# Layer norm on three engines and sooner, in the output stage of a spectral mixer

## The chip, the cores and the metric

The kernel runs on one core of one Trainium2 chip. The metric is the device time of one execution in microseconds. A median over several executions is given; the profile is of one execution, with its own time.

## The reference

Two layers, each of a spectral mixer (A) and a channel MLP (B), on one sequence of 2048 rows by 576 columns:

```python
def _A_ref(x, w_r, w_i):
    X = rfft2(x.astype(float32), axes=(-2, -1))
    X = X * (w_r + 1j * w_i)
    return irfft2(X, s=(S, D)).astype(bfloat16)

def _B_ref(x, w1, b1, w2, b2):
    y = _layernorm(x)                       # over the 576 columns
    h = gelu(einsum("bsd,df->bsf", y, w1) + b1)   # 4608 wide
    return einsum("bsf,fd->bsd", h, w2) + b2

for _ in range(2):
    x = x + _A_ref(_layernorm(x), A_w_r, A_w_i)
    x = x + _B_ref(_layernorm(x), B_w1, B_b1, B_w2, B_b2)
```

The part that concerns us is the seam between the mixer and the MLP: the last step of the inverse transform gives the new x, tile by tile, and the MLP's first matrix product wants the layer norm of the first 512 rows of that x, transposed.

## The kernel before

The 2048 rows lie in SBUF as 16 tiles of 128 partitions and 576 columns (`x_sb`). The tiles are worked in four quads, `QUADS = [[j, j+4, j+8, j+12] for j in range(4)]`, and `order` lists the tiles quad after quad. The output stage numbers them n = 0 to 15 in that order, so the first quad is n = 0 to 3.

Every engine executes its instructions in the order in which the program lists them (`manual_schedule`); nothing reorders them. What an engine does is therefore decided by the order of the calls in `SpectralOut.run_all`. That stage occurs twice, once in each layer. For each n it issues, in this order:

- `put_x(n)`, only for n = 6 and 10 (n = 1 and 2 are done ahead): TensorE adds x itself into PSUM with four matmuls (L753). These four tiles are called early.
- `idft_k(n)`: six matmuls of 288 columns (L765), into a PSUM tile `psb` of which there are three (tag "big").
- `add(n)`: VectorE forms the new x. For an ordinary tile it is one "even" add of 576 columns (L785), which writes a float32 tile `tt`, and two "odd" adds of 288 columns (`add_odd`, L793 and L794), which write x and after which the PSUM tile is free. The odd adds of tile n-1 follow the even add of tile n, unless n is early. For an early tile ScalarE copies half of the PSUM tile (L777) and VectorE makes two adds (L779).
- what `behind_add[n]` lists,
- `idft_v(n + 2)`: four matmuls (L698) and a ScalarE copy from PSUM (L705), for the tile after next; once in four tiles also `idft_v_rest` (L738, L745),
- what `pieces[n]` lists.

`Prep` is the layer norm of the first quad, which is worked while the later tiles are still being added. `sum(i, k)` are eight ScalarE passes (L845) that accumulate the sum and the sum of squares of tile i. `moments` are three small VectorE instructions (L854 to L856), `root` one ScalarE square root (L860), `scale_sums` two small VectorE instructions (L865, L866). `norm(i)` is one VectorE instruction of 576 columns (L887) that writes `xn`, and `norm_act(i)` the same on ScalarE (L874). Each is followed by a copy of the last 64 columns behind the 576 (L890 on VectorE, L877 on POOL), so that five transposes of 128 columns fill the width. There are three `xn` buffers. `turn(i, "act")` makes five transposes on TensorE (L907) into a PSUM tile `pss`, and one ScalarE copy of 640 columns (L909) to `yT`.

The `pss` tiles (tag "sm") number two. `idft_v`, `idft_v_rest` and `turn` take them in turn, so a transposition can begin only when the ScalarE copy of the last but one user has ended.

The lists before:

```python
pieces[10].append(prep.root)
for i, m in enumerate((13, 14, 14)):
    pieces[m].append(lambda i=i: prep.turn(i, "act"))
behind_add = {9: [prep.moments], 11: [prep.scale_sums, lambda: prep.norm(0, nc.vector)], 12: [lambda: prep.norm(2, nc.vector)]}
pieces[12].append(lambda: prep.norm_act(1))
pieces[13].append(lambda: prep.norm_act(3))
...
    if n == NT - 1:
        prep.turn(3, "act")
```

After n = 15, `mlp_up` begins: matmuls of 512 columns (L931) that read `yT` of all four tiles, and PSUM tiles of the same three `psb` that the adds of tiles 13, 14 and 15 have to free. POOL (GpSimd) issues the exchange DMAs of the stage before, the 64-column copies, one memset for the next mixer (L1122, first layer alone) and the loads of w2 (L265), the latter only after the MLP's first activations.

Of the kernel before, what the change touches and what calls it, by code (L numbers as in the profile page):

```python
# [11 lines left out]
ALU = mybir.AluOpType  # L12
BF16 = mybir.dt.bfloat16
# [4 lines left out]
S, D = 2048, 576  # L18
P = 128
NT = 16  # L20
# [141 lines left out]
def kernel(  # L162
# [12 lines left out]
    nc = tc.nc  # L175
# [8 lines left out]
    work = ctx.enter_context(tc.tile_pool(name="work", bufs=2))  # L184
# [24 lines left out]
    def at(buf, shape, off=0):  # L209
        n = int(np.prod(shape[1:]))  # L210
        dims = "abcd"[: len(shape) - 1]
        return buf[0 : shape[0], off : off + n].rearrange(f"p ({' '.join(dims)}) -> p {' '.join(dims)}", **dict(zip(dims[1:], shape[2:])))

    x_sb = persist.tile([P, NT, D], BF16, name="x_sb")
# [123 lines left out]
    def ln_scale(mv, mlp, sqrt):  # L338

        n = mv.shape[1]  # L340
        rs = work.tile([P, n], F32, tag="ln_rs", bufs=4)
        if sqrt:
            sq = work.tile([P, n], F32, tag="ln_v")
            nc.scalar.activation(
                out=sq[:], in_=mv[:, :, 1], func=ACT.Sqrt, bias=c_eps[:, 1:2] if mlp else c_eps[:, 0:1], scale=(1.0 + EPS) if mlp else 1.0
            )
            nc.vector.reciprocal(out=rs[:], in_=sq[:])
            return [(mv[:, i, 0:1], rs[:, i : i + 1]) for i in range(n)]
        vv = work.tile([P, n], F32, tag="ln_v")
        hv = work.tile([P, n], F32, tag="ln_hv")  # L350
        tt = work.tile([P, n], F32, tag="ln_t")
        sc, add = (1.0 + EPS, EPS * EPS) if mlp else (1.0, EPS)
        nc.vector.tensor_scalar(out=vv[:], in0=mv[:, :, 1], scalar1=sc, scalar2=add, op0=ALU.mult, op1=ALU.add)
        nc.vector.tensor_scalar(out=hv[:], in0=vv[:], scalar1=-0.5, scalar2=None, op0=ALU.mult)
        nc.vector.tensor_scalar(
            out=rs[:].bitcast(I32), in0=vv[:].bitcast(I32), scalar1=-0.5, scalar2=1597463007.0, op0=ALU.mult, op1=ALU.add
        )
        for _ in range(3):
            nc.vector.tensor_mul(out=tt[:], in0=rs[:], in1=rs[:])
            nc.vector.tensor_mul(out=tt[:], in0=tt[:], in1=hv[:])  # L360
            nc.vector.scalar_tensor_tensor(out=rs[:], in0=tt[:], scalar=1.5, in1=rs[:], op0=ALU.add, op1=ALU.mult)
        return [(mv[:, i, 0:1], rs[:, i : i + 1]) for i in range(n)]
# [321 lines left out]
    class SpectralOut:  # L684
# [84 lines left out]

        def add(self, n):  # L770

            if n > 0 and n - 1 not in self.early and n in self.early:
                self.add_odd(n - 1)
            if n in self.early:
                xr, po = x_sb[:, order[n], :].rearrange("p (h n) -> p h n", h=2), self.st.pop(("po", n))
                odd = at(self.sums, [P, DH], 2 * DH * (n % 3))
                nc.scalar.copy(out=odd, in_=po[:, 1, 0:DH])  # L777
                for half, op in ((0, ALU.add), (1, ALU.subtract)):
                    nc.vector.tensor_tensor(out=xr[:, half], in0=po[:, 0, 0:DH], in1=odd, op=op)  # L779
                return  # L780
            if n < NT:
                t, po = order[n], self.st["po", n]
                tt = at(self.sums, [P, 2, DH], 2 * DH * (n % 3))
                xr = x_sb[:, t, :].rearrange("p (h n) -> p h n", h=2)
                nc.vector.tensor_tensor(out=tt, in0=po[:, 0:1, 0:DH].to_broadcast([P, 2, DH]), in1=xr, op=ALU.add)  # L785
                self.st["tt", n] = tt
            if n > 0 and n - 1 not in self.early:
                self.add_odd(n - 1)

        def add_odd(self, n):  # L790
# [5 lines left out]
        def run_all(self, prep, loads):  # L796

            pieces = {n: [] for n in range(NT)}
            for n, (i, k) in zip((1, 2, 3, 4, 5, 5, 6, 7), ((i, k) for i in range(4) for k in range(2))):
                pieces[n].append(lambda i=i, k=k: prep.sum(i, k))  # L800
            pieces[10].append(prep.root)
            for i, m in enumerate((13, 14, 14)):
                pieces[m].append(lambda i=i: prep.turn(i, "act"))
            behind_add = {9: [prep.moments], 11: [prep.scale_sums, lambda: prep.norm(0, nc.vector)], 12: [lambda: prep.norm(2, nc.vector)]}
            pieces[12].append(lambda: prep.norm_act(1))
            pieces[13].append(lambda: prep.norm_act(3))
            for n in self.early[:2]:
                self.put_x(n)
            for n in range(N_FIRST):
                self.idft_v_late(n)  # L810
            self.idft_v_rest_late()
            self.idft_v(0)
            for call in loads:
                tc.add_manual_dep(call(), marks["u2", 0].name, SYNC, reason="pace of the loads")
            self.idft_v(1)
            self.idft_v_rest(0)
            self.idft_v(2)
            for n in range(NT):
                if n == NT - 1:
                    prep.turn(3, "act")  # L820
                if n in self.early[2:]:
                    self.put_x(n)
                self.idft_k(n)
                self.add(n)
                for call in behind_add.get(n, ()):
                    call()
                if 0 < n < NT - 2:
                    self.idft_v(n + 2)
                if n % 4 == 1 and n + 3 < NT:
                    self.idft_v_rest(n // 4 + 1)  # L830
                for call in pieces[n]:
                    call()
            self.add(NT)

    class Prep:
# [35 lines left out]
        def norm_act(self, i):  # L871
            rs, shift = self.rs_shift
            xn = work.tile([P, 640], BF16, tag="xn", bufs=3)
            nc.scalar.activation(  # L874
                out=xn[:, 0:D], in_=x_sb[:, self.quad[i], :], func=ACT.Identity, bias=shift[:, i : i + 1], scale=rs[:, i : i + 1]
            )
            nc.gpsimd.tensor_copy(out=xn[:, D:640], in_=xn[:, D - 64 : D])  # L877
            self.st[i] = xn
# [185 lines left out]
    for n, (kind, j) in enumerate(early):  # L1064
        i = 1 + 5 * n // 8
# [21 lines left out]
    for li in range(N_LAYERS):  # L1087
# [24 lines left out]
        prep = Prep(0, sqrt=True)  # L1112
# [47 lines left out]
```

## Time and profile before

| what | us |
|---|---|
| median of 3 runs | 730.78 (730.43 to 731.42) |
| the profiled execution: its own time | 730.14 |
| the profiled execution: span from first to last instruction | 728.4 |
| TensorE busy in the span | 716.3 (98%) |
| ScalarE busy / VectorE busy / POOL busy | 309.3 / 266.9 / 79.3 |
| layer 0: first L765 matmul, first L931 matmul | 61.52, 84.82 |
| layer 1: L931 matmul after the output stage | 439.61 |

Span and time of the profiled execution differ by 1.7 us, which lies around the instructions. In the profile's rows the name left of `<-` is what is written and the names right of it what is read; the bracket at the end of a row gives the engine's idle time before it and what ended it. Matmuls are pipelined, so their duration reaches beyond the start of the next; the spacing of starts is what a matmul costs. PE is TensorE and PEld its weight load, DVE is VectorE, ACT is ScalarE, POOL is GpSimd, SP the engine that issues DMAs.

In the trace, n = 9 to 15 of layer 0 are psb_1330, 1371, 1395, 1418, 1441, 1468 and 1499, and psb_1513 is the first of the MLP.

### The profile page before, as it was taken

The numbers are of one execution on the slowest core, as the hardware profiler recorded it, in microseconds if no ns is written. First come the engines' busy times: TensorE is split into PE (matmuls) and PEld (weight loads), VectorE is DVE, ScalarE is ACT, GpSimd is POOL, SyncE is SP. The second block draws the span as 40 slices with busy tenths as digits, with TensorE's granted clock in tenths as the row PEclk, the third lists the DMA queues.
The fourth block names the chain that finished last, engine by engine and source line by source line (L and its number), as shares of the span: only waits on it lengthen the run. The fifth ranks groups of instructions, "written<-read, shape, count | busy, mean of one in ns | idle before, by whom it ended". The sixth has DMA issues, their size and how long they took to land.

```text
span 728.4 us, 12438 instructions
## 1 busy us (share of the span) xinstructions
PE 716.3 (98%) x5044; PEld 457.1 (63%) x5078; DVE 266.9 (37%) x917; ACT 309.3 (42%) x534; POOL 79.3 (11%) x139
## 2 busy tenths in 40 slices
PE   9999999999999999999999999999999999999998
PEld 5777645864587448744877774477447744774476
DVE  7894910664055504520366586011400140110011
ACT  7796764026411651156216686610550056005600
POOL 4240112002000200000106201200100010000000
PEclk9999999999999999999999999999999999999999
DMA  9787345211112111100217402530102010100000
GB/s 297 209 194 208 135 152 193 65 44 54 37 36 54 55 27 45 46 8 1 59 37 232 140 2 74 191 110 18 44 1 45 17 45 1 45 21 6 1 17 17
DMA packets 52722, 54.33 MB, mean 75 GB/s; under 512 B 31576, under 2 KB 43624, under 8 KB 52664
## 3 DMA queue, kind: packets, MB, share of 16 engines
q1 hardware_dynamic: 43784, 25.99, 13.3%
q0 software_dynamic: 8448, 26.96, 11.7%
q8 instruction: 40, 0.66, 0.4%
q10 hardware_dynamic: 432, 0.58, 0.2%
q14 instruction: 18, 0.15, 0.1%
HBM read 29.31 MB, written 8.59 MB: 52 GB/s over the span
## 4 chain that ended last, share of the span: by engine, by line
PE 95%; ACT 2%; DVE 1%; issue 1%; DMA 0%; ACTq 0%
PE psb_4485 L978 1%; PE psb_3601 L978 1%; PE psb_7498 L978 1%; PE psb_6900 L978 1%; PE psb_6302 L978 1%; PE psb_3472 L978 1%; PE psb_2799 L978 1%; PE psb_1997 L978 1%; PE psb_1758 L978 1%; PE psb_7652 L978 1%; PE psb_7575 L978 1%; PE psb_7183 L978 1%; PE psb_7106 L978 1%; PE psb_7028 L978 1%; PE psb_6585 L978 1%; PE psb_6508 L978 1%
## 5 line engine op out<-in xcount | busy, mean ns | idle before, releaser
L978 PEld LDWEIGHTS <-h_sb 128*128 128x128 bf16 x2304 | 224.9, 98 | 57.8 <-issue 0.2
L931 PEld LDWEIGHTS <-w_sb 128*128 128x128 bf16 x1152 | 109.4, 98 | 142.4 <-issue 17.2
L887 DVE TENSOR_SCALAR xn<-x_sb,mv,rs 128x576 bf16<-128x576 bf16 x24 | 9.4, 427 | 67.0 <-DMA quad_1817<-xn 28.9
L335 DVE BATCH_NORM_STATS2 stats<-x_sb 128x6 f32<-128x288 bf16 x78 | 30.8, 437 | 0.0
L939 PEld LDWEIGHTS <-w1r_sb 64*128 64x128 bf16 x288 | 10.8, 94 | 24.5 <-issue 17.0
L973 DVE TENSOR_TENSOR xb<-x_sb,b_bc 128x576 f32<-128x576 bf16 x32 | 24.0, 749 | 0.0
L890 POOL COPY xn<-xn 128x64 bf16<-128x64 bf16 x24 | 6.4, 266 | 150.8 <-DVE xn L887 150.8
L656 PEld LDWEIGHTS <-h_sb 128*128 128x128 bf16 x160 | 15.4, 97 | 5.3 <-DVE shared_721 L641 0.5
L945 ACT ACTIVATE h_sb<-psb_6062,b_sb 128x512 bf16<-128x512 f32 x2 | 1.3, 684 | 37.9 <-PE psb_6062 L939 37.9
L945 ACT ACTIVATE h_sb<-psb_6660,b_sb 128x512 bf16<-128x512 f32 x2 | 1.3, 684 | 37.8 <-PE psb_6660 L939 37.8
L945 ACT ACTIVATE h_sb<-psb_7258,b_sb 128x512 bf16<-128x512 f32 x2 | 1.3, 684 | 37.8 <-PE psb_7258 L939 37.8
L1001 DVE TENSOR_TENSOR x_sb<-psb_7498,xb 128x576 bf16<-128x576 f32 x1 | 0.8, 759 | 43.4 <-PE psb_7498 L978 43.4
L1001 DVE TENSOR_TENSOR x_sb<-psb_4099,xb 128x576 bf16<-128x576 f32 x1 | 0.8, 757 | 39.5 <-PE psb_4099 L978 39.5
L417 DVE TENSOR_TENSOR xf<-ef 128x256 bf16<-128x256 f32 (+1 forms) x56 | 13.6, 305 | 0.5
L623 PEld LDWEIGHTS <-c_f_84 128*128 128x128 bf16 x108 | 10.4, 97 | 4.6 <-issue 1.6
L1001 DVE TENSOR_TENSOR x_sb<-psb_6900,xb 128x576 bf16<-128x576 f32 x1 | 0.8, 757 | 33.6 <-PE psb_6900 L978 33.6
L1001 DVE TENSOR_TENSOR x_sb<-psb_6302,xb 128x576 bf16<-128x576 f32 x1 | 0.8, 758 | 33.6 <-PE psb_6302 L978 33.6
L504 PEld LDWEIGHTS <-c_k_82 128*128 128x128 bf16 x112 | 10.4, 98 | 2.3
L1001 DVE TENSOR_TENSOR x_sb<-psb_3293,xb 128x576 bf16<-128x576 f32 x1 | 0.8, 758 | 28.7 <-PE psb_3293 L978 28.7
L1001 DVE TENSOR_TENSOR x_sb<-psb_2491,xb 128x576 bf16<-128x576 f32 x1 | 0.8, 757 | 28.7 <-PE psb_2491 L978 28.7
L845 ACT ACTIVATE h_sb<-x_sb 128x576 bf16<-128x576 bf16 x16 | 11.2, 700 | 0.1
L488 PEld LDWEIGHTS <-xT 128*128 128x128 bf16 x96 | 9.2, 97 | 3.1 <-issue 0.7
(1420 smaller groups left out, 1530.5 us busy)
## 6 DMA issues: line engine op xcount, KB each, us to landing
w_sb<-in_B_w_dram SPq DMA_DIRECT2D x16, 288.0 KB
v_sb<-in_B_w_dram POOLq DMA_DIRECT2D x4, 1152.0 KB, 6.1
shared_1511<-in_B_w_dram POOLq DMA_DIRECT2D x2, 1440.0 KB, 7.4
shared_5459<-in_B_w_dram POOLq DMA_DIRECT2D x2, 1440.0 KB, 7.5
out_dram<-x_sb SPq DMA_DIRECT2D x15, 144.0 KB
v_sb<-w_sb POOLq DMA_DIRECT2D x13, 145.0 KB, 4.8
x_sb<-in_A_x_dram SPq DMA_DIRECT2D x3, 576.0 KB
b_sb<-shared_721 POOLq DMA_DIRECT2D x11, 145.0 KB, 5.0
```

The costliest lines, as they stand in the source:

```text
L335: nc.vector.bn_stats(out=stats[:, h, :], in_=x_sb[:, t, h * DH : (h + 1) * DH])
L417: nc.vector.tensor_tensor(out=xf[:, at0 : at0 + 2 * n].rearrange("p (g d) -> p g d", g=2), in0=ef[:, :, first : first + n], in1=ef[:, :, b ...
L488: nc.tensor.matmul(pz[:, o, 0:KP], lhsT=xT[:, ci, :], rhs=c_fd[:, 3 * o + q, :], start=(q == 0), stop=(q == 2),)
L504: nc.tensor.matmul(py[:, r, 0:KP], lhsT=(c_k1_late if t in LATE else c_k1)[:, pl, :], rhs=z[:, ri], start=(q == 0), stop=(q == 1))
L623: nc.tensor.matmul(px[:, o, 0:KP], lhsT=c_f2[:, n // 4, pl, n % 4, :], rhs=vx[:, E_SLOTS.index(e), ri, :], start=(q == 0), stop=(q == 1))
L656: nc.tensor.matmul((ph, odd)[o][:, o, 0:KP], lhsT=i1[:, pl, n % 4, :], rhs=rhs, start=(q == 0), stop=(q == len(terms) - 1))
L845: nc.scalar.activation(out=at(h_sb, [P, D], 512 * 34), in_=x_sb[:, self.quad[i], :], func=(ACT.Copy, ACT.Square)[k], accum_out=self.s12[:, ...
L887: nc.vector.tensor_scalar(out=xn[:, 0:D], in0=x_sb[:, self.quad[i], :], scalar1=mean, scalar2=rs, op0=ALU.subtract, op1=ALU.mult)
L931: nc.tensor.matmul(acc[p][q], lhsT=w1_sb[:, ci, fc * 128 : (fc + 1) * 128], rhs=yT[:, ci, :], start=(first and ci == 0), stop=(not first a ...
L939: nc.tensor.matmul(acc[p][q], lhsT=w1r_sb[rows, p, :], rhs=yT[rows, 4, :], start=first, stop=not first)
L973: nc.vector.tensor_tensor(out=xb[:], in0=xr, in1=b2_bc[:].rearrange("p (h n) -> p h n", h=2), op=ALU.add)
L978: nc.tensor.matmul(parts[h][:, h, 0:DH], lhsT=hts[fc][:, i * 128 : (i + 1) * 128], rhs=w2_chunk(fc)[:, h * DH : (h + 1) * DH], start=(fc = ...
```

## The change

The lists are written anew, a third kind of norm is added, and the odd adds of two late tiles are moved.

```diff
         def add(self, n):
-            if n > 0 and n - 1 not in self.early and n in self.early:
+            odd_first = n in self.early or n >= NT - 2
+            if n > 0 and n - 1 not in self.early and odd_first:
                 self.add_odd(n - 1)
...
-            if n > 0 and n - 1 not in self.early:
+            if n > 0 and n - 1 not in self.early and not odd_first:
                 self.add_odd(n - 1)
...
-            pieces[10].append(prep.root)
-            for i, m in enumerate((13, 14, 14)):
-                pieces[m].append(lambda i=i: prep.turn(i, "act"))
-            behind_add = {9: [prep.moments], 11: [prep.scale_sums, lambda: prep.norm(0, nc.vector)], 12: [lambda: prep.norm(2, nc.vector)]}
-            pieces[12].append(lambda: prep.norm_act(1))
-            pieces[13].append(lambda: prep.norm_act(3))
+            behind_add = {8: [prep.moments], 9: [prep.scale_sums, lambda: prep.norm(0)]}
+            pieces[8].append(prep.root)
+            pieces[10] += [lambda: prep.norm_act(2), lambda: prep.norm_pool(1)]
+            for n, i in ((11, 0), (12, 2), (13, 1), (14, 3)):
+                pieces[n].append(lambda i=i: prep.turn(i, "act"))
+            pieces[11].append(lambda: prep.norm_act(3))
...
             for n in range(NT):
-                if n == NT - 1:
-                    prep.turn(3, "act")
...
+        def norm_pool(self, i):
+            mean, rs = self.mr[i]
+            xn = work.tile([P, 640], BF16, tag="xn", bufs=3)
+            nc.gpsimd.tensor_scalar(
+                out=xn[:, 0:D], in0=x_sb[:, self.quad[i], :], scalar1=mean, scalar2=rs, op0=ALU.subtract, op1=ALU.mult
+            )
             nc.gpsimd.tensor_copy(out=xn[:, D:640], in_=xn[:, D - 64 : D])
             self.st[i] = xn
```

- The moments come behind the adds of n = 8 instead of 9, the root after n = 8 instead of 10, the scale behind n = 9 instead of 11.
- The norms: tile 0 on VectorE behind n = 9 (before: n = 11), tile 2 on ScalarE after n = 10 (before: VectorE, n = 12), tile 1 on POOL after n = 10 (before: ScalarE, n = 12), tile 3 on ScalarE after n = 11 (before: n = 13).
- All four 64-column copies are on POOL; before, those of tiles 0 and 2 were on VectorE.
- The turns come one at a time, after n = 11, 12, 13 and 14, for tiles 0, 2, 1, 3. Before, tile 0 was turned after n = 13, tiles 1 and 2 after n = 14 and tile 3 ahead of `idft_k(15)`, which is the same place on TensorE as the end of n = 14.
- For n = 14 and 15 the odd adds of the tile before come ahead of the even add of the tile itself.

In the built program of the changed kernel, POOL's list for one layer is: copy (tile 0), copy (tile 2), norm (tile 1), copy (tile 1), copy (tile 3). In the first layer alone, one more POOL instruction that the source does not spell stands just ahead of that norm, under the same line number. It is a reload of a GpSimd library (`PseudoReloadLibraryIndex`, index 0). The kernel before has no such instruction.

More of the change, by code (lines that the diff above doesn't have):

```diff
@@ L875, in norm_act @@
                 out=xn[:, 0:D], in_=x_sb[:, self.quad[i], :], func=ACT.Identity, bias=shift[:, i : i + 1], scale=rs[:, i : i + 1]
+            )
+            nc.gpsimd.tensor_copy(out=xn[:, D:640], in_=xn[:, D - 64 : D])
+            self.st[i] = xn
+        def norm_pool(self, i):
[3 more added lines that the diff above has]
+                out=xn[:, 0:D], in0=x_sb[:, self.quad[i], :], scalar1=mean, scalar2=rs, op0=ALU.subtract, op1=ALU.mult
             )
```

## The prediction

> **What bounds the kernel now.** I read the page first, then the chain of waits around the seam, then TensorE's timeline there.
>
> ```profile
> PE 716.3 (98%) x5044; PEld 457.1 (63%) x5078; DVE 266.9 (37%) x917; ACT 309.3 (42%) x534; POOL 79.3 (11%) x139
> PE 95%; ACT 2%; DVE 1%; issue 1%; DMA 0%; ACTq 0%
> ```
>
> TensorE holds 95% of the chain that ended last. So a gain or a loss at the seam reaches the end one for one: what follows is a queue of matmuls, and its loads are paced by activations that move with it. ScalarE's 2% is where the seam shows. The chain of waits at the first layer's seam (start, us, what):
>
> ```profile
> 79.78 0.59 ACT u_1436 L705
> 80.37 0.55 ACT xn L874
> 80.92 0.12 issue
> 81.04 0.26 ACT u_1456 L705
> 81.30 0.21 issue
> 81.50 0.70 ACT yT_1407 L909
> 82.20 0.77 ACT xn L874
> 82.97 1.81 ACT yT_1407 L909 x3
> 84.78 0.04 issue
> 84.82 0.38 PE psb_1513 L931
> ```
>
> From 79.78 to 84.82 ScalarE sets the pace: it holds two norms and four turn copies at the very end. TensorE in the same stretch:
>
> ```profile
> 80.70 0.44 PE L907 MATMUL pss_1458<-ident,xn 128*128 128x128 bf16 x5
> 81.27 0.40 PE L765 MATMUL psb_1468<-c_gd,u_1436 128*128 128x288 bf16 x2
> ...
> 82.28 0.44 PE L907 MATMUL pss_1485<-ident,xn 128*128 128x128 bf16 x5
> 83.60 0.44 PE L907 MATMUL pss_1492<-ident,xn 128*128 128x128 bf16 x5 [0.88 <-ACT yT_1407 L909]
> 83.88 0.41 PE L765 MATMUL psb_1499<-c_gd,u_1456 128*128 128x288 bf16 x2
> ```
>
> By spacing of starts a turn costs 0.28 (82.00 to 82.28, 83.60 to 83.88), an `idft_k` 0.73 and an `idft_v` 0.44. Idle: about 0.29 before 81.27 (the psb tile of n = 11 is freed by VectorE's odd adds, end 81.22), 1.04 before 83.60 (the pss tile is freed by a turn copy that ends at 83.55), and 0.21 before 84.82 (the last turn copy ends at 84.77). Together **1.54 us**; layer 1 is the same row for row (turn at 438.39 after 0.88, MLP at 439.61). The change can win at most 2 x 1.54 = 3.1.
>
> **What the Trainium skill says.** GPSIMD Engine Reference, "2.1 Instruction dispatch": the first call to a freshly loaded GpSimd kernel also pays an IRAM load of about 6 us (5.95 measured there), with no instruction for it in the profile. The trace before shows no such load. The same page, "3.1 Elementwise — side-by-side cycle accounting": bodies of up to two operations run at 1.03 cycles an element, a two-input body at 2.6. No row of POOL here does arithmetic; these are its nearest (a memset, then a 64-column copy):
>
> ```profile
> 2.23 1.06 POOL L278 MEMSET b_sb<- 128x1160 bf16 x1
> 83.03 0.24 POOL L877 COPY xn<-xn 128x64 bf16<-128x64 bf16 x1 [1.60 <-ACT xn L874]
> ```
>
> TensorE: Matmul & The Clock Gate, "Part 1: The HAM clock gate": the array falls to half rate after an idle window of about 3.4 us and needs as long a busy one to return. The trace agrees on two rates: five 512-column matmuls at the start take 2.32 us, seven at 57 us take 1.69 (though the page's clock row reads full speed throughout):
>
> ```profile
> 1.01 2.32 PE L257 MATMUL pss_127<-zeros 128*128 128x512 bf16 x5 [1.01 <-DVE h_sb L287]
> 57.26 1.69 PE L257 MATMUL psb_1068<-zeros 128*128 128x512 bf16 x7
> ```
>
> **The change part by part**, in layer 0's times; TensorE's order up to `idft_v(13)` at 77.92 is the old one.
>
> *Moments, root, scale sooner.* On VectorE the three moments cost 0.56 of slots and now begin at 74.84, behind the odd adds that ended there. The variance is there at 75.48. ScalarE's root waits for that behind `idft_v(10)`'s copy (free at 74.63), from 75.5 to 75.85. Queued behind it are the copies of `idft_v(11)` (before at 75.10, now 75.8) and of the rest (76.3). TensorE needs them at 77.08 and 78.48, and the first one's pss tile at 76.63 (free at 76.4): hidden, by 0.2 at the narrowest. Lost cover would cost what is over. Scale and norm 0 then start at about 76.8 and end at 77.5 (before: 78.91 to 79.61).
>
> *VectorE.* It loses one norm (slot 0.46) and two copies (0.10 each): 0.66 a layer. Its backlog before is real (the even add of n = 13 starts at 81.72, its matmuls end about 80.4), and the 0.29 idle above came from it. With the new order I get odd(11) done at 81.1, when `idft_k(14)` asks at 82.0. So that wait goes.
>
> *Copies on POOL.* 0.24 each in place of VectorE's 0.18; POOL waits from 54.8 on for nothing else. The copy of tile 0 at about 77.6 to 77.85, turn 0 wants it at 78.36: hidden. POOL's later work (memset L1122, w2 loads behind the first activations at 88.8) has room; no DMA is issued more or fewer, and none changes its place on SP's queue.
>
> *ScalarE and the turns.* ScalarE's count is unchanged (two norms of 0.77, four turn copies of 0.6 spacing); their place is not. Walking both queues: turn 0 at 78.36; its copy at 79.17 (behind norm 2, 77.92, and a copy), done 79.87; so turn 2 at 79.92, norm 3 from 79.76, the `idft_v(14)` copy 80.53 to 81.12, so `idft_v(15)` at 81.17 (0.24 late), turn copy 2 81.01 to 81.71, so **turn 1 at 81.76** (0.15 late), `idft_k(14)` 82.04, turn 3 82.77, `idft_k(15)` 83.05 to 83.78, last turn copy 83.27 to 83.97 and the MLP at **84.02**. Before: 84.82. That is **-0.80 a layer**; of 1.54 idle, 0.74 stays, now spread.
>
> *Odd sums first for n = 14, 15.* No instruction more. The psb tile of n = 13 is free at about 83.4 (MLP wants it at 84.02), that of n = 14 at 84.8 (wanted 85.75). With the old order n = 14's would come at about 85.5: still hidden, barely. I cost this at nothing, with VectorE's remaining backlog as the cover.
>
> *Norm 1 on POOL.* It needs scale (77.1) and comes behind the copy of tile 2, which ends at about 79.1. Length: the memsets' slope (1.55 for 1740, 1.06 for 1160) is 0.84 ns an element, and a 64-column copy of 0.24 leaves 0.19 fixed: 0.67; the two-input price of that page, at its 1.2 GHz and with the same 0.19, gives 1.4. I take 0.7, by the nearest rows. With its own copy it ends by 80.1, and turn 1 asks at 81.76: hidden with 1.7 to spare in layer 1. That holds up to a norm of 2.4.
>
> *The library reload, layer 0.* It stands between the copy of tile 2 and norm 1. Nothing here shows its length L. Lower bound 0 (already resident, or loaded in the shadow); below nothing is excluded, for it does no work of the kernel. Upper, by judgement, twice the page's price. I take 6. Then norm 1 starts at 79.1 + 6 = 85.1, ends 85.8, its copy 86.05, and turn 1 starts at about **86.1 instead of 81.76**. Queued behind it on TensorE are `idft_k(14)`, turn 3, `idft_k(15)` and the whole MLP: 84.02 + 4.34 = 88.36, which is **+3.54** against 84.82. In general layer 0 gives L - 2.46 once L is over 1.66, and -0.80 below.
>
> **Sum**: +3.54 - 0.80 = **+2.74** on the profiled execution's 730.14, so 732.9. The median shown is 0.64 above that execution; I put the same difference on it: **733.5**.
>
> **Rivals.**
> 1. *The reload costs nothing on the path* (L under 1.66). For: POOL has been idle for 23 us, DMA is at 3 GB/s from 80 to 84. Against: POOL takes its list in order, and the reload is listed behind two copies that wait. Then both layers gain 0.80: **729.2**. The forecast turns into it at L = 3.26, where the two layers cancel.
> 2. *The reload is long, or it costs TensorE its clock.* At L = 6 TensorE stands from 81.61 to 86.1, 4.5 us, longer than the page's window. At half rate for some 3.4 us it does half the work, about +1.7; with L = 10, +6.7, and with both +8.4: **737 to 739**.
> 3. *POOL's norm is far slower than 2.4 us.* Both layers lose: at 4 us, 1.6 late each, less the 0.80: +0.8 a layer, without any reload 732.4. Against: copies and memsets at 0.84 ns an element.
> 4. *ScalarE still sets the end and nothing moves* (waits as long as before, 730.8): the walk shows narrow margins, but the idle has to be 0.8 longer than I find.
>
> **How the numbers follow.** Forecast (L from about 4 to 8): 0.50, its own range 731.5 to 736. Rival 1: 0.24. Rival 2: 0.22. Rivals 3 and 4: 0.02 each. A measurement of this kernel can tell about 0.2%, 1.5 us, from no change: 729.3 to 732.2. Rival 1 sits at that edge; I split it, 0.13 faster and 0.11 same. Rival 4 and the short end of L add 0.03 to same. Slower is the rest: 0.73. The range takes rival 1 in with 0.2 to spare at the bottom, and L of 10 with the clock lost and a slower POOL norm at the top: 729.0 to 741.0.
>
> **What would show it.** Right: in layer 0 norm 1 on POOL starts some 6 us after the copy of tile 2, turn 1 near 86 with an idle of over 4 us ended by POOL, MLP at 88.4; in layer 1 norm 1 starts right behind that copy, no TensorE idle over 0.3, MLP about 0.8 sooner after `idft_v(13)` (now 6.9 later). VectorE no longer ends a wait of TensorE. Wrong: norm 1 right behind the copy in layer 0 too (rival 1), matmuls at twice the spacing after the wait (rival 2), or a POOL norm over 2.4 us in both layers (rival 3).

## The result, and the profile after

The change makes the kernel faster, by about 0.25%: a median of **728.8 us** (728.46 to 730.14, 6 runs) against 731.1 (730.34 to 732.75, 6 runs) on the same chip, ratio 0.9971 (95% interval 0.9957 to 0.9985). A second measurement on another occasion gave 729.03 against 730.76 (12 and 27 runs), ratio 0.9975 (0.9967 to 0.9984). The forecast was 733.5, slower, with a range of 729.0 to 741.0. What came is its rival 1, "the reload costs nothing on the path", put at 729.2 and 0.24.

The profiled execution took 728.46 us, 1.68 less than the one before. To see where, I use one measure throughout: the **seam**, from the start of `idft_v(13)` on TensorE to the first matmul of the MLP. Before, it is 77.92 to 84.82 and 432.71 to 439.61: 6.90 in both layers. After, it is 78.25 to 84.31 and 431.88 to 437.94: **6.06 in both layers**. Two times 0.84 is the 1.68. That the two agree to the hundredth is luck: ahead of layer 0's seam the changed kernel is 0.33 later (its output stage already begins at 61.86, before at 61.52), between the two seams it gains 0.32, and these cancel.

TensorE's timeline after, at the seam of layer 0 (start, us, engine, line, what is written and read):

```profile
78.69 0.44 PE L915 MATMUL pss_1424<-ident,xn 128*128 128x128 bf16 x5
...
79.70 0.60 PE L698 MATMUL pss_1444<-c_r_85,b_sb 128*128 128x256 bf16 x4
80.24 0.44 PE L915 MATMUL pss_1451<-ident,xn 128*128 128x128 bf16 x5
...
81.48 0.60 PE L698 MATMUL pss_1468<-c_r_85,b_sb 128*128 128x256 bf16 x4
82.07 0.44 PE L915 MATMUL pss_1475<-ident,xn 128*128 128x128 bf16 x5
...
83.08 0.44 PE L915 MATMUL pss_1492<-ident,xn 128*128 128x128 bf16 x5
...
84.31 1.89 PE L939 MATMUL psb_1513<-yT_1351,w_sb 128*128 128x512 bf16 x8
```

The turns stand one at a time between other work. With the spacings of before (0.44, 0.28, 0.73), turn 2 is 0.10 late, `idft_v(15)` 0.23, turn 1 0.15 and the MLP 0.22: 0.70 idle in place of 1.54. The 1.04 that was lost ahead of the last turn is gone.

POOL after, in the same stretch:

```profile
77.96 0.24 POOL L898 COPY xn<-xn 128x64 bf16<-128x64 bf16 x1 [22.88 <-DVE xn L895]
79.18 0.24 POOL L876 COPY xn<-xn 128x64 bf16<-128x64 bf16 x1 [0.98 <-PE pss_1424 L915]
79.49 2.28 POOL L882 TENSOR_SCALAR xn<-x_sb,mean,rs 128x576 bf16<-128x576 bf16 x1
81.84 0.24 POOL L885 COPY xn<-xn 128x64 bf16<-128x64 bf16 x1
```

Two things stand here that the forecast had otherwise. From the copy's end (79.42) to the norm's start, where the reload stands, only **0.07 us** pass, not 6. (In layer 1, without a reload, the norm starts 0.22 after the start of the copy; here it is 0.31. So the reload cost about 0.09.) And the norm took **2.28 us**, not 0.7.

### The profile page after: what moved, and what is told of

Same layout as the page of the kernel before. It is cut to its first block, busy times and chain, and to the rows that moved or that the text cites. A ratio compares the mean times of both kernels' runs of the same rounds, so it can differ in the third digit from the quotient of the medians.

```text
span 726.7 us, 12472 instructions
## 1 busy us (share of the span) xinstructions
PE 718.2 (99%) x5078; PEld 456.6 (63%) x5078; DVE 265.7 (37%) x911; ACT 308.8 (42%) x534; POOL 84.8 (12%) x145
## 4 chain that ended last, share of the span: by engine, by line
PE 93%; DVE 2%; ACT 2%; DMA 1%; issue 1%; SPq 1%; POOL 0%; POOLq 0%; ACTq 0%; DVEq 0%
PE psb_4485 L986 1%; PE psb_3729 L986 1%; PE psb_3601 L986 1%; PE psb_3472 L986 1%; PE psb_2799 L986 1%; PE psb_1997 L986 1%; PE psb_7652 L986 1%; PE psb_7575 L986 1%; PE psb_7498 L986 1%; PE psb_7183 L986 1%; PE psb_7106 L986 1%; PE psb_7028 L986 1%; PE psb_6900 L986 1%; PE psb_6585 L986 1%; PE psb_6508 L986 1%; PE psb_6430 L986 1%
```

## The experiments

Each is the changed kernel with one edit, unless it says otherwise. Most ran once. The profile gives the seam to some 0.05 us (6.06 or 6.07 wherever the seam's code is that of the changed kernel). The time of single executions of one kernel varies by 1 to 2.6 us; the stretch between the two seams, which no edit touches, alone took from 347.6 to 349.0. So the seam decides.

**Was the reload free because the library was there?** A POOL instruction of another library is put in first, so that this one has to be fetched again:

```diff
+            if <layer 0>:                       # at the start of the output stage
+                ...                             # pq, pw: scratch tiles of 4 columns
+                nc.gpsimd.memset(pq[:], 1.0)
+                nc.gpsimd.partition_broadcast(pw[:], pq[:])
+                nc.gpsimd.tensor_copy(out=pq[:], in_=pw[:])
             for n in self.early[:2]:
                 self.put_x(n)
```

> The changed kernel, with one POOL partition_broadcast of 4 columns at the start of layer 0's output stage, which belongs to another GpSimd library, so that another library is resident when the reload ahead of norm 1 is reached. Theory (in the changed kernel the reload named the library that was resident already and loaded nothing): here the broadcast and then norm 1 each start some 6 us late; norm 1 starts 6 after the copy of tile 2 instead of 0.07, the seam of layer 0 is about 12, the time 5 to 6 above the changed kernel's. Rival (a reload is always this cheap, or is done ahead): norm 1 still starts within 0.3 of the copy, seam 6.06.

Measured: POOL's timeline (the reloads have no row of their own here; the bracket holds them):

```profile
55.13 0.12 POOL L811 MEMSET libq<- 128x4 f32 x1
61.19 0.28 POOL L812 PARTITION_BROADCAST libw<-libq  x1 [5.94 <-issue]
...
79.23 0.24 POOL L884 COPY xn<-xn 128x64 bf16<-128x64 bf16 x1 [0.99 <-PE pss L923]
87.05 2.30 POOL L890 TENSOR_SCALAR xn<-x_sb,mean,rs 128x576 bf16<-128x576 bf16 x1 [7.58 <-issue]
```

Ahead of the broadcast POOL stands 5.94, and ahead of norm 1 it stands **7.58**, in both cases waiting for nothing that the profile shows. The same reload ahead of the same norm costs 0.07 when no other library was loaded before it. So in the changed kernel its library was resident: the two runs together show it. What had put it there before the first instruction is not seen in a trace. The seam of layer 0 became 14.68, that of layer 1 stayed 6.06, the execution took 737.92. My number for the seam (12) was low for two reasons: the reload was 7.6, and the clock fell (0.50 granted from 87 to 91).

**What would a late norm have cost?** Two further POOL norms hold norm 1 back in layer 0:

```diff
         def norm_pool(self, i):
             mean, rs = self.mr[i]
             xn = work.tile([P, 640], BF16, tag="xn", bufs=3)
+            for _ in range(2 if <layer 0> else 0):
+                nc.gpsimd.tensor_scalar(out=xn[:, 0:D], ...)   # as below
             nc.gpsimd.tensor_scalar(
```

> The changed kernel, with two further POOL norms (same operands, into the same xn buffer, overwritten by the real one) ahead of norm 1 in layer 0 alone: they hold norm 1 back by 2 x 2.28 = 4.6 us, as a reload of that length would have. Measure: from the start of idft_v(13) to the first MLP matmul (6.90 before, 6.06 after, both layers). My account: turn 1 of layer 0 starts 4.6 later than in the changed kernel, the seam of layer 0 is 10.6, that of layer 1 stays 6.06, the time is 4.6 above the changed kernel's, and TensorE keeps its rate. Rival (clock): TensorE stands[...] and then runs at half rate, 512-column matmuls spaced 0.43 instead of 0.22 for some us, seam and time a further 1.5 to 2 longer. Rival (slack): part of the hold is covered, turn 1 moves by less than 3.5.

Measured: norm 1 began 6.02 after `idft_v(13)`, against 1.24: held by 4.78. Turn 1 began 8.36 after it, against 3.82: 4.54 later. So only 0.24 of the hold was covered, and in the changed kernel the norm had that much to spare. The rows around it, and then TensorE's stretches (the columns are busy us and instructions of PE, PEld, DVE, ACT and POOL, then the granted TensorE clock, DMA share, GB/s):

```profile
83.95 2.29 POOL L888 TENSOR_SCALAR xn<-x_sb,mean,rs 128x576 bf16<-128x576 bf16 x1
...
86.29 0.53 PE L921 MATMUL pss<-ident,xn 128*128 128x128 bf16 x5 [4.53 <-POOL xn L888]
86.66 0.62 PE L765 MATMUL psb<-c_gd,u 128*128 128x288 bf16 x2
```

```profile
77.90:81.50 3.60, 3.53 (x36) 2.81 (x34) 3.53 (x8) 3.60 (x7) 2.52 (x2) 1.00 0.25 91
81.50:86.20 4.70, 0.26 (x3) 0.00 (x0) 1.84 (x5) 0.79 (x2) 4.54 (x2) 1.00 0.00 0
86.20:90.00 3.80, 3.71 (x22) 2.55 (x23) 1.58 (x3) 1.87 (x3) 2.00 (x4) 0.57 0.00 0
90.00:94.00 4.00, 3.95 (x20) 1.73 (x21) 3.69 (x9) 0.80 (x1) 0.00 (x0) 0.98 0.02 4
```

After 4.5 us of standing, the clock is 0.57 for the next 3.8. From turn 1 to the MLP it takes 3.71 in place of 2.24: 1.47 more. The seam is 12.07, 735.61 the time. The rival on the clock is right and my own number (10.6) misses that part. In the experiment with the other library the same stretch was 1.33 longer after 7.3 us of standing.

**How slow is arithmetic on POOL, and is VectorE the reason?** The edit adds POOL instructions on scratch tiles after the last MLP up stage; these seven are the ones measured:

```diff
+                ...                                # scratch tiles pa, pb, and a memset of pa
+                for n in (576, 288, 64):
+                    nc.gpsimd.tensor_scalar(out=pb[:, 0:n], in0=pa[:, 0:n], **two)
+                nc.gpsimd.tensor_scalar(..., scalar1=pr, scalar2=None, op0=ALU.mult)
+                nc.gpsimd.tensor_scalar(..., scalar1=0.5, scalar2=2.0, ...)
+                nc.gpsimd.tensor_copy(out=pb[:, 0:D], in_=pa[:, 0:D])
+                nc.gpsimd.tensor_scalar(..., **two)
```

> The changed kernel, with POOL instructions on scratch tiles after the last MLP up stage of layer 1, where VectorE is almost idle: tensor_scalar of 576, 288 and 64 columns with two operations and scalars per partition, 576 with one operation, 576 with immediate scalars, a copy of 576, and the first form once more. Theory (POOL arithmetic is slow by itself, some 3.6 ns an element over 0.2 fixed): 576 takes 2.28 again, 288 about 1.25, 64 about 0.45, one operation less or equal, the copy of 576 about 0.7. Rival[...]: 576 falls to 0.7 to 1.4 here, where VectorE is quiet.

```profile
L1025 POOL TENSOR_SCALAR probe<-probe,mv,rs x3: 582/1329/2287, 595.2 to 599.0; 128x576 bf16<-128x576 bf16 x1, 128x288 bf16<-128x288 bf16 x1, 128x64 bf16<-128x64 bf16 x1
```

```profile
599.71 1.73 POOL L1026 TENSOR_SCALAR probe<-probe,rs 128x576 bf16<-128x576 bf16 x1
601.53 2.15 POOL L1027 TENSOR_SCALAR probe<-probe 128x576 bf16<-128x576 bf16 x1
603.74 0.66 POOL L1028 COPY probe<-probe 128x576 bf16<-128x576 bf16 x1
```

The first row gives shortest, middle and longest of the three widths: 0.58, 1.33 and 2.29. (2287 - 582) / 512 is 3.3 ns a column over 0.37 fixed. One operation instead of two saves a quarter, immediate scalars nearly nothing. The copy of the same width is 0.66, which is what I had priced the norm at. VectorE ran nothing from 593.3 to 610 and the norm took as long as in the seam, so VectorE was not the cause.

**What is the third engine worth?** Two kernels take the arithmetic off POOL.

```diff
-            behind_add = {..., 9: [prep.scale_sums, lambda: prep.norm(0)]}
+            behind_add = {..., 9: [prep.scale_sums, lambda: prep.norm(0)], 10: [lambda: prep.norm(1)]}
-            pieces[10] += [lambda: prep.norm_act(2), lambda: prep.norm_pool(1)]
+            pieces[10] += [lambda: prep.norm_act(2)]
```

> The changed kernel with norm 1 on VectorE, behind the adds of n = 10, and only its copy on POOL: no POOL arithmetic, no reload. My account: turn 1 is held by two things that end together at 82.03 to 82.08 in layer 0, the copy of turn 2 on ScalarE and norm 1 with its copy on POOL; so taking POOL's part away wins at most 0.05 to 0.1 a layer, seam 5.95 to 6.06, if VectorE's further 0.36 stays hidden. Rival A (POOL's norm is what sets the end): seam 5.8 or less. Rival B (VectorE has no room): its odd adds hold a PSUM tile and the seam is 6.2 or more.

```diff
-            behind_add = {..., 9: [prep.scale_sums, lambda: prep.norm(0)]}
+            behind_add = {..., 9: [prep.scale_sums, lambda: prep.norm(0, nc.vector)], 10: [lambda: prep.norm(2, nc.vector)]}
-            pieces[10] += [lambda: prep.norm_act(2), lambda: prep.norm_pool(1)]
+            pieces[10] += [lambda: prep.norm_act(1)]
```

> The changed kernel with the norms on the engines of before (0 and 2 on VectorE with their copies, 1 and 3 on ScalarE) but at the new places, and the turns spread. No POOL arithmetic. My account: ScalarE's queue is the same, VectorE has about 0.6 more, which frees the PSUM tile for idft_k(15) about 0.2 late; seam (idft_v(13) to the MLP) 6.05 to 6.3, so nearly the whole gain stays. Rival (the third engine is what pays): the seam is 6.6 or more.

Measured: norm 1 on VectorE gives a seam of 6.06 in both layers, every start on TensorE where it was. The engines of before, at the new places, give 6.12 and 6.07. So POOL's norm, which the page's chain of the changed kernel runs through, does not set the end: without it the same turn waits for the pss tile, as long (0.15). Nearly the whole gain is there with two engines.

**Which of the moves makes the gain?** Without the last part:

```diff
-            odd_first = n in self.early or n >= NT - 2
+            odd_first = n in self.early
```

> The changed kernel without its last part: for n = 14 and 15 the even add comes first again. The prediction held this part to be worth nothing. Walking VectorE's queue in the trace after: the even add of n = 14 can start only at about 83.3 in layer 0, then the odd adds of n = 13 end at 84.8 instead of 83.7, and the first MLP matmul (84.31) waits for their PSUM tile: seam 6.5, about 0.5 a layer longer, and VectorE ends the wait before the MLP. Prediction's view: seam stays 6.06.

```profile
83.22 0.76 DVE L786 TENSOR_TENSOR shared<-psb,x_sb 128x576 f32<-128x576 f32 x1 [0.35 <-PE psb L765]
83.90 0.45 DVE L794 TENSOR_TENSOR x_sb<-shared,psb 128x288 bf16<-128x288 f32 x1
84.26 0.45 DVE L795 TENSOR_TENSOR x_sb<-shared,psb 128x288 bf16<-128x288 f32 x1
```

```profile
84.85 1.46 PE L939 MATMUL psb<-yT,w_sb 128*128 128x512 bf16 x5 [0.65 <-DVE x_sb L795]
```

The seam is 6.66 and 6.58. VectorE stands 0.35 for the matmuls of n = 14 while the odd adds of n = 13 lie behind, and the MLP then waits for the PSUM tile that those free. Leaving out this one part costs 0.60 and 0.52, about **0.56 a layer**, two thirds of the gain. It can only be so much because the turns now end sooner: in the kernel before, n = 13's PSUM tile was free at 84.59 and the last turn copy ended at 84.77, so there, by this reading, the part would have won nothing; that was not run.

With the turns at their old places:

```diff
-            for n, i in ((11, 0), (12, 2), (13, 1), (14, 3)):
+            for n, i in ((13, 0), (14, 2), (14, 1), (14, 3)):
-            pieces[11].append(lambda: prep.norm_act(3))
+            pieces[13].append(lambda: prep.norm_act(3))
```

> The changed kernel with its norms where they are, but the turns at the places of before (tile 0 after n = 13, tiles 2, 1 and 3 after n = 14), and norm 3 after n = 13, because its buffer is that of tile 0. My account: the spreading of turns, not the early norms, makes the gain, since two pss tiles and one ScalarE queue take the turns one by one: seam 6.7 to 6.9. Rival (norms that are done early are enough): seam 6.3 or less.

```profile
83.81 0.44 PE L915 MATMUL pss<-ident,xn 128*128 128x128 bf16 x5 [0.91 <-ACT yT L917]
```

The seam is 6.90 and 6.83: the wait of before is back, 0.91 for a turn copy. On ScalarE norm 3 stands ahead of that copy again:

```profile
82.31 0.87 ACT L873 ACTIVATE xn<-x_sb,shift,rs 128x576 bf16<-128x576 bf16 x1
83.08 1.90 ACT L917 COPY yT<-pss 128x640 bf16<-128x640 bf16 x3
```

So this run takes back two things at once: the turns' places, and norm 3's place on ScalarE. It has to, because norm 3 writes the buffer that turn 0 reads. An estimate from these rows: without norm 3 there, the copy of turn 2 could start at about 82.4 instead of 83.08, and some 0.7 of the wait would go. The early turn of tile 0 may therefore pay mainly by letting norm 3 leave the end of ScalarE's queue. A kernel that parts the two (late turns, early norm 3, a fourth buffer) was not run.

And the kernel before, with only moments, root and scale moved:

```diff
-            pieces[10].append(prep.root)
+            pieces[8].append(prep.root)
-            behind_add = {9: [prep.moments], 11: [prep.scale_sums, lambda: prep.norm(0, nc.vector)], ...}
+            behind_add = {8: [prep.moments], 9: [prep.scale_sums], 11: [lambda: prep.norm(0, nc.vector)], ...}
```

> The kernel before, with only the moments, the root and the scale at their new places; norms and turns as before. My account: these are not on the path, seam 6.9 (6.8 to 7.0) in both layers. Rival (the statistics hold the norms): seam 6.6 or less.

6.91 in both layers. So early statistics win nothing by themselves; they let the turns and norm 3 spread, the spread takes the 1.04 away, and the odd adds keep VectorE from giving most of it back. The parts do not add up: leaving out either of the last two loses most of the gain or all of it.

**A version that beats both?** First norms 1 and 3 on POOL, with norm 0's copy on VectorE; then that copy on ScalarE.

```diff
-            behind_add = {..., 9: [prep.scale_sums, lambda: prep.norm(0)]}
+            behind_add = {..., 9: [prep.scale_sums, lambda: prep.norm(0, nc.vector)]}
-            pieces[10] += [lambda: prep.norm_act(2), lambda: prep.norm_pool(1)]
+            pieces[9].append(lambda: prep.norm_pool(1))
+            pieces[10].append(lambda: prep.norm_act(2))
-            pieces[11].append(lambda: prep.norm_act(3))
+            pieces[11].append(lambda: prep.norm_pool(3))
```

> The changed kernel with norms 1 and 3 both on POOL (norm 1 as soon as the scale is there, norm 3 after it), norm 2 alone on ScalarE, norm 0 and its copy on VectorE. ScalarE loses 0.77 in the seam, VectorE gains 0.1, POOL's two norms end at about 79.8 and 82.6 in layer 0. My account (ScalarE's copies hold the pss tiles, POOL has room): idft_v(15) and turn 1 no longer wait, seam 5.7 to 5.8 instead of 6.06 in both layers, time 0.5 to 0.7 below the changed kernel's, ratio to before about 0.996. Rival A (POOL is now late): turn 3 waits for norm 3, seam 6.0 or more. Rival B (VectorE's odd adds set idft_k(15)): seam 5.9 to 6.1.

> The changed kernel once more, on the same chip, for comparison: seam 6.06 in both layers, ratio to before about 0.997.

Measured: seams 5.98 and 5.80 against 6.06 and 6.07; 728.79 (16 runs) against 729.03, both with before at 730.76, ratios 0.9973 (0.9966 to 0.9981) and 0.9975 (0.9967 to 0.9984). Rival B is part of it. VectorE's 64-column copy stretched while POOL's norm ran:

```profile
77.15 2.44 POOL L883 TENSOR_SCALAR xn<-x_sb,mean,rs 128x576 bf16<-128x576 bf16 x1 [22.39 <-DVE rs L865]
```

```profile
77.54 0.60 DVE L899 COPY xn<-xn 128x64 bf16<-128x64 bf16 x1
78.06 0.44 DVE L794 TENSOR_TENSOR x_sb<-shared,psb 128x288 bf16<-128x288 f32 x1
```

It took 0.60 (0.52 in layer 1). In the kernel with the engines of before, at the same place but with no POOL norm, it took 0.18 in both layers. The odd adds of n = 12 ended at 83.04, when `idft_k(15)` could have begun at 82.86. The next edit, against the kernel just shown, takes that copy off VectorE:

```diff
-            ... prep.norm(0, nc.vector)
+            ... prep.norm(0, None)                 # the norm alone
-            pieces[10].append(lambda: prep.norm_act(2))
+            pieces[10] += [lambda: prep.tail_act(0), lambda: prep.norm_act(2)]   # tail_act: nc.scalar.copy of the 64 columns
```

> The kernel with norms 1 and 3 on POOL, with the 64-column copy of tile 0 moved from VectorE to ScalarE, ahead of norm 2. In that kernel VectorE's copy took 0.60 and 0.52 instead of 0.18 while POOL's norm ran, and idft_k(15) then waited for VectorE's odd adds. Theory[...]: VectorE is 0.4 to 0.6 earlier, idft_k(15) no longer waits, seam 5.7 to 5.8 in both layers, time 0.2 to 0.4 lower again. Rival (the copy was waiting for norm 0's own end, not for POOL): VectorE gains only the 0.1 slot, seam 5.9 in layer 0.

Measured: the odd adds that followed at 78.06 start at 77.42, `idft_k(15)` no longer waits, seam 5.82 in both layers: 0.16 shorter in layer 0, while layer 1 (5.80) wins nothing. The time is 728.88 (7 runs) against before 730.97, ratio 0.9971 (0.996 to 0.9983). By the seams this version is 0.5 us below the changed kernel; the intervals of the times overlap, so a gain over the changed kernel in time is not shown.

The last run asks whether VectorE's instructions stretch beside a POOL norm away from the seam too:

```diff
+                ...                                # scratch tiles pa, pb, pc, and a memset of pa
+                nc.gpsimd.tensor_scalar(out=pb[:, 0:D], in0=pa[:, 0:D], **two)
+                for _ in range(4):
+                    nc.vector.tensor_copy(out=pc[:, 0:64], in_=pa[:, 0:64])
+                nc.vector.tensor_scalar(out=pc[:, 0:D], in0=pa[:, 0:D], **two)
+                ...                                # the same five behind POOL's end
```

> The changed kernel, with a probe after the last MLP up stage: four VectorE copies of 64 columns and a VectorE norm of 576, all bfloat16, started together with a POOL norm of 576 (2.28 alone); then the same five once POOL has finished. [...]the first group takes 0.4 to 0.6 a copy and more than 0.42 for the norm, or POOL's norm takes longer than 2.28; the second group takes 0.18 and 0.42. Rival: both groups alike.

Inconclusive: VectorE reached its group only at 653.0, long after POOL's norm (594.23 to 596.52), so nothing overlapped, and both groups took 0.18 and 0.43. What stands is that the copy is long where POOL's norm runs beside it and short where there is none; by what means is not settled.

## Why the prediction was wrong, step by step

- **The step that failed: "The library reload, layer 0 ... I take 6."** Where a library really has to come, the price is of that size (5.94 and 7.58 here, 5.95 in the Trainium skill's GPSIMD Engine Reference, "2.1 Instruction dispatch"). The condition was not met: that section speaks of a freshly loaded kernel, and I named the lower bound ("already resident") without a reason to prefer the page's price. The reload took 0.07, so layer 0's +3.54 became -0.84.
- **"Norm 1 on POOL ... I take 0.7"**: 2.28. The nearest rows, copies and memsets, do not price arithmetic; a copy of 576 columns is 0.66. The two-input price of the same page, "3.1 Elementwise — side-by-side cycle accounting", gave 1.4, also too low; its 1.03 cycles for up to two operations, at its 1.2 GHz, give an estimate of 0.86 ns a column, and 3.3 were measured. The measurement decides. By luck the cover that I named held: hidden up to 2.4.
- **"Odd sums first ... I cost this at nothing"**: 0.56 a layer. I walked the PSUM tile of n = 14 under the old order (85.5 against 85.75) and that of n = 13, which the MLP wants first, only under the new one (83.4). The new order is thus in the walk that gave -0.80, and the sum is not off by this; what I had wrong is that nothing hangs on it.
- **The gain without the reload**: -0.80 a layer forecast, -0.84 measured. The idle left was forecast as 0.11, 0.24, 0.15 and 0.24 at its four places, and is 0.10, 0.23, 0.15 and 0.22. Walking the queues row by row was accurate to a few hundredths. For rival 1 this gives 728.54 on the profiled execution (730.14 less 1.60); it took 728.46, helped by the luck told above.
- **Cover for the moments**: `idft_v(12)`'s tile was freed in time, no wait of TensorE there; root at 75.84 after the 0.77 wait of ScalarE, as walked.
- **Rival 2, the clock**: not met in the changed kernel, but right as a price. At 4.5 us of standing I said 1.7; in the experiment with the hold it was 1.47. The clock of 0.57 over the 3.8 us that followed agrees with the Trainium skill's TensorE: Matmul & The Clock Gate, "Part 1: The HAM clock gate" (half rate after an idle window of about 3.4 us, and about as long a busy one to return).
- **Rival 3** needed a norm over 2.4 us, and 2.28 is only 0.1 below. By the experiment with the hold the norm had 0.24 to spare, so some 2.5 was the limit.

With the reload as the trace shows it (0.07), the working of the prediction gives its rival 1. What turned the sign was one input and the weight on it; the walk of the path held, although the norm's length in it was three times too small.

## What to carry to other kernels

When an instruction of unknown length stands on the path, ask first whether its cost is due at all in this program, then price it; an experiment that makes it due by force tells both. Where several things wait for the same two buffers and one queue, look at spreading them over the stage first: here that gained, and a faster norm 1 did not. The next engine in line then has to be given the order that frees what is asked for first. A wait that two causes end together shows one of them in the chain; taking that one away, as here with POOL's norm, can change nothing.

## What I had not expected of the hardware

- A library reload with its library resident took 0.07 us between two POOL instructions; with another resident, 5.94 and 7.58.
- POOL's tensor_scalar on bfloat16 runs at 3.3 ns a column over 0.37 us, with scalars from memory or immediate (2.29 and 2.15 for 576); a copy of the same width takes 0.66.
- A turn's first transposes start on the norm alone: in the kernel with the hold, TensorE began at 86.29, and the copy of the last 64 columns ran from 86.30.
- A 64-column copy on VectorE took 0.52 to 0.60 instead of 0.18 beside a POOL norm, and that norm 2.44 instead of 2.28. The norm's 2.44 is not the copy's doing: it took as long with that copy on ScalarE (2.44 and 2.43), and VectorE's own norm of tile 0 ran beside its start in both kernels. The cause is open.
